# Two tiles of a weight fold laid between the products of neighbouring MLP units, and a planner that lets ScalarE's operations overlap

## The chip, the core and the metric

The kernel runs on one core of one Trainium2 chip. The metric is device microseconds of that core, from the first instruction to the last, inputs and output in HBM. The matrix engine is TensorE (PE in the profile), the others are VectorE (DVE), ScalarE (ACT), GpSimd (POOL) and SyncE (SP), whose queue starts the DMAs.

## What is computed

One token block of 2048 rows and 640 columns passes through a layer norm. On the result stand a linear attention with 32 heads of width 20 and a gated MLP with 1536 hidden columns; both are added to the input.

```python
xn = _layernorm(x)
# A: linear attention; phi is a softmax of p and of -p, side by side
q, k, v = split(xn @ wqkv)                      # 32 heads of 20
pq, pk = q @ w_phi, k @ w_phi                   # per head
phi = concat([softmax(p), softmax(-p)])
kv = einsum("bhsf,bhsd->bhfd", phi_k, v);  z = phi_k.sum(over s)
A = ((phi_q @ kv) / (phi_q @ z + 1e-6)) @ wo
# B: MLP
B = ((silu(xn @ w1)) * (xn @ w3)) @ w2
out = x + A + B
```

## The kernel before

Everything stays on the chip between load and store; the tokens are 16 tiles of 128 rows. The steps of the kernel are written as streams (generators): layer norm (`norms`), transposes, the key fold (`fold_k`), value and key tiles (`attention`), key norms, queries and their followers, MLP units (`mlps`) and output tiles (`outs`). A planner, the loop at the end of the kernel, picks again and again the step that can start first by its own book of due times, and appends its operations to each engine's list. So the order of the work follows from `_Program.commit`, which writes down when each operation ends (`o.end`) and when its engine is free (`self.free`), from fixed costs per operation. Engines run their lists in order and wait for each other by semaphores. A DMA's list is SP's queue.

PSUM has 8 banks, used as four pairs. `banks(2)` gives the pair whose last user ends first, leaving out pairs in `held`.

**The fold.** The per-head matrix `w_phi` is multiplied into the key and query weights, so that a key tile is one projection: `fold_mm(which, dc, k)` makes rows 128 dc to 128 dc + 127 of the folded weight `Wkp` (keys) or `Wqp` (queries) by six products of the transposed weight `wqkT` with the block diagonal `BDc`, four of 140 columns and two of 80, into a bank pair, and copies the pair out (`evac`, to ScalarE or VectorE, whichever the book has free first). One such call is called a fold tile here. `fold_k` issues the key fold's five tiles in a row, and key tiles wait for them (`done["f"]`).

**An MLP unit** (`mlp(b, fc, k)`) computes 128 hidden columns for 512 tokens: five products of 512 columns with `w1` into bank k, five with `w3` into bank k + 1, then ScalarE's `th` (tanh of the first bank), VectorE's `t` (which reads the first bank again) and VectorE's `hT` (which reads `t` and the second bank). There are 48; units 0 to 3 are the first four, before the other weights are loaded.

**A key tile** is ten products of 320 columns with `Wkp` and two exponentials on ScalarE into `ekt`; VectorE then sums and GpSimd scales `ekt`. **A value tile** is ten products with `wv` and one copy on ScalarE. From tile 4 on a value tile follows each key tile (called v tile 4 and so on), and between tiles 9 and 13 a fold tile of the queries follows as well. The layer norm of tiles 4 to 15 is applied (`x_tok`) on VectorE or ScalarE by the book, and SP's DMA transposes bring them into `xnT`, the operand of all projections.

Before the change, the order of TensorE round the fold is: value tiles 0 to 3, units 0 and 1, the five fold tiles, unit 2, key tiles 0 to 3, unit 3, key tile 4, v tile 4, and so on.

Of the kernel before, what the change touches and what calls it, by code (L numbers as in the profile page):

```python
# [3 lines left out]
ACT = mybir.ActivationFunctionType  # L4
ALU = mybir.AluOpType
# [9 lines left out]
DC = D // 128  # L15
# [10 lines left out]
def heads_of_chunk(c):  # L26
    return (128 * c) // DH, (128 * c + 127) // DH
# [16 lines left out]
class _Program:  # L44
# [127 lines left out]
    def commit(self, ops):  # L172
        for o in ops:
            o.idx = len(self.ops)
            o.deps = self.find_deps(o)
            t = self.free[o.eng]
            for d in o.deps:
                t = max(t, d.end + (0.03 if d.eng == o.eng else 0.07))
            o.start = t
            if o.dma:  # L180
                self.free[o.eng] = t + 0.45
                if "T" == o.part:
                    self.free[o.eng] = t + (1.28 if o.cost < 5e5 else o.cost / 105e3)
                self.bus = max(self.bus, t + 0.5) + o.cost / (280e3 if o.part else 305e3)
                if o.part and o.cost > 5e5:
                    self.bus = max(self.bus, self.free[o.eng] + 1.0)
                o.end = self.bus + (1.5 if t < 1 else 1.6 if t < 3.5 or o.part and o.cost < 2e5 else 2.6)
            else:
                o.end = t + o.cost
                self.free[o.eng] = o.end  # L190
            self.ops.append(o)
            if o.eng == "POOL" and not o.dma:
                self.pool = o
            for g in o.reads:
                if isinstance(g, tuple):
                    self.bank.setdefault(g, {})[o.eng] = o
                else:
                    self.last_r.setdefault(g, {})[("dma", o.idx) if o.dma else o.eng] = o
            for g in o.writes:
                if isinstance(g, tuple):  # L200
                    self.bank.setdefault(g, {})[o.eng] = o
                else:
                    self.last_w[g] = o
                    self.last_r.pop(g, None)
# [45 lines left out]
def bass_parallel_sum__linear_kernel_hedgehog__glu_gated_swiglu__prompt_kernel(  # L250
# [29 lines left out]
    def new(name, shape, dtype, offset=None):  # L280
        size = mybir.dt.size(dtype)
        for n in shape[1:]:
            size *= n
        return P.sbuf(name, shape, dtype, region(size) if offset is None else offset)
# [17 lines left out]
    th = new("th", [128, 3, 512], f32)  # L302
    t1 = new("t1", [128, 3, 512], bf)
# [40 lines left out]
    def bank(k, cols=512, off=0, rows=128):  # L344
        return PS[0:rows, k * 512 + off:k * 512 + off + cols]

    def bank2(k, cols):
        return PS[:, k * 512:(k + 2) * 512].rearrange("p (b c) -> p b c", c=512)[:, :, 0:cols]


    def mm(o, l, r, start, stop, shared=False, cost=None):
        n = free(r)
        P.op("PE", "matmul", [o], [l, r], (o, l, r),
             dict(start=start, stop=stop, skip_group_check=shared),
             cost=max(n / 2400 + 0.003, 0.055) if cost is None else cost)
# [5 lines left out]
    def free(ap):  # L361
        n = 1
        for s in ap.shape[1:]:
            n *= s
        return n

    def act(o, i, f, scale=1.0):
        P.op("ACT", "activation", [o], [i], (o, i, f), dict(scale=scale),
             cost=0.17 + free(o) / 1200)
# [5 lines left out]
    def stt(o, a, s, b, f0, f1):  # L375
        P.op("DVE", "scalar_tensor_tensor", [o], [a, b], (),
             dict(out=o, in0=a, scalar=s, in1=b, op0=f0, op1=f1), cost=0.16 + free(o) / 960)

    def copy(eng, o, i, fast=1):
        if eng == "ACT":  # L380
            act(o, i, ACT.Copy)
        else:
            P.op(eng, "tensor_copy", [o], [i], (o, i), cost=0.14 + free(o) / 960 / fast)

    def evac(o, i):

        a = P.free["ACT"] + 0.17 + free(o) / 1200
        d = P.free["DVE"] + 0.14 + free(o) / 960 / (2 if i.dtype == bf else 1)
        copy("ACT" if a <= d else "DVE", o, i, 2 if i.dtype == bf else 1)
# [143 lines left out]
               phi_s[:, c, :].unsqueeze(1).to_broadcast([128, n, DH]),  # L533
               GM[:, c, h0:h1 + 1].unsqueeze(2).to_broadcast([128, n, DH]), ALU.mult)

    def fold_mm(which, dc, k):
        first = [True, True]
        for e in range(DC):
            h0, h1 = heads_of_chunk(e)
            lo, hi = DH * h0, DH * (h1 + 1)  # L540
            for q in range(2):
                a, b = max(lo, 320 * q), min(hi, 320 * q + 320)
                if a < b:
                    mm(bank(k + q, b - a, a - 320 * q), wqkT[:, which * DC + e, 128 * dc:128 * dc + 128],
                       BDc[:, e, a - lo:b - lo], first[q], e == DC - 1 or (q == 0 and e == 2), True)
                    first[q] = False
        dst = (Wqp, Wkp)[which]
        evac(dst[:, dc, :].rearrange("p (b c) -> p b c", c=320), bank2(k, 320))


    def part(w, t, q, i, k, off=0):
        mm(bank(k + q, 320, 0 if q else off), xnT[:, i, t * 128:(t + 1) * 128], w[:, i, 320 * q:320 * q + 320],
           i == 0, i == DC - 1)
# [6 lines left out]
    def v_store(t, k):  # L560
        pv = PS[:, k * 512 + 192:k * 512 + 192 + 60 * NG].rearrange("p (g h c) -> p g h c", h=3, c=DH)
        act(v_heads(v2[:, t, :])[:, :, :, 0:DH], pv, ACT.Copy)

    def v_tile(t, k):
        proj(t, wv, k, 192)
        v_store(t, k)
# [107 lines left out]

    nmlp = [0]

    def mlp(b, fc, k):
        n = nmlp[0] % 3
        nmlp[0] += 1
        for w, kk in ((w1_s, k), (w3_s, k + 1)):  # L680
            for i in range(DC):
                mm(bank(kk), w[:, i, fc * 128:(fc + 1) * 128], xnT[:, i, b * 512:(b + 1) * 512],
                   i == 0, i == DC - 1)
        act(th[:, n, :], bank(k), ACT.Tanh, 0.5)
        stt(t1[:, n, :], th[:, n, :], 1.0, bank(k), ALU.add, ALU.mult)
        stt(hT[b][:, fc, :], t1[:, n, :], 0.5, bank(k + 1), ALU.mult, ALU.mult)

    finish = []
# [26 lines left out]
    held = set()  # L715

    def banks(n):

        def free_at(k):
            return max([o.end for i in range(k, k + n) for o in P.bank.get(("P", i), {}).values()],  # L720
                       default=0.0)
        return min((k for k in range(0, 8, n) if k // 2 not in held), key=free_at)

    done = dict.fromkeys(("w", "ln", "t", "f", "k", "n", "kv", "v", "u", "qp", "qn", "qd", "q", "o", "h", "v0", "bd"), 0)
# [40 lines left out]
            todo = [t, t + 1]  # L765

    def fold_k():
        while not done["bd"]:
            yield None
        for dc in range(DC):  # L770
            yield lambda dc=dc: fold_mm(1, dc, banks(2))
        done["f"] += 1

    done["w"] = 4

# [35 lines left out]
    def attention():  # L811
        def v(t):
            return lambda: v_tile(t, banks(2))

        yield warm_up
        for t in range(4):
            while done["t"] <= t:
                yield None
            k = banks(2)
            held.add(k // 2)  # L820
            for q in range(2):
                for i in range(DC):
                    if t == 0 and q == 1:
                        while done["t"] < 2:
                            yield None
                    yield lambda t=t, q=q, i=i, k=k: part(wv, t, q, i, k, 192)
                    done["v0"] += 1
            yield lambda t=t, k=k: v_store(t, k)
            held.clear()
        while done["f"] < 1:  # L830
            yield None
        for t in range(T):
            while done["t"] <= t:
                yield None
            yield lambda t=t: k_tile(t, banks(2))
            done["k"] = t + 1
            if t >= 4:
                yield v(t)
            if 9 <= t < 14:
                yield lambda dc=t - 9: fold_mm(0, dc, banks(2))  # L840
        yield lambda: P.dma("SP", wo_s[:], A_wo.rearrange("(c p) d -> p c d", p=128))
        done["v"] = 1
# [54 lines left out]
    def o_transposes():  # L897
        for t in range(T):
# [2 lines left out]
            yield lambda t=t: P.dma("SP", oT[:, :, t * 128:(t + 1) * 128], o_tok[:, t % 3, 0:D], True)  # L901
            done["o"] = t + 1

    def mlps():
        for b in range(NB):
            for fc in range(FC):
                while done["t"] < 4 * b + 4 or done["w"] <= fc or b == 2 and done["t"] < T or b == 3 and not done["kv"]:
                    yield None
                yield lambda b=b, fc=fc: mlp(b, fc, banks(2))
                done["u"] = 12 * b + fc + 1  # L910
            done["h"] = b + 1

    def outs():
# [10 lines left out]
    n = len(streams)  # L924
    heads, alive = [None] * n, [True] * n
    while any(alive):
# [32 lines left out]
        i, ops, after = best[2:]  # L959
# [65 lines left out]
```

## Time and profile before

| | |
|---|---|
| time, median of 3 runs | 268.69 us (268.46 to 268.83) |
| the profiled execution | 268.28 us, its span 266.6 us |
| TensorE busy | 261.6 us, 1938 matmul records, 1959 weight loads |
| VectorE, ScalarE, GpSimd busy | 168.8, 98.8, 100.6 us |
| granted TensorE clock | 1.00 throughout |

How to read it: a row of the timeline gives the start and the duration in us, the engine, the line, the operation, output and inputs, and how many operations were merged into it; in brackets stands idle time of the engine before it and what ended it. Nearly every operation is issued by one helper at line 102, so rows are told apart by the names of their tiles: `PS<-BDc,wqkT` is the fold, `PS<-xnT,w_s` an MLP unit, `PS<-Wkp,xnT` a key tile, `PS<-wv,xnT` a value tile. PEld is TensorE's weight load, which goes on beside the products. Matmul ends are modelled and reach over the start of the next one, so distances are taken from start to start; some matmul records are missing.

### The profile page before, as it was taken

What the parts mean: (1) busy time and instruction counts of PE and PEld (TensorE: products, weight loads), DVE (VectorE), ACT (ScalarE), POOL (GpSimd) and SP (SyncE); (2) the same over time, 40 slices, a digit from 0 to 9 for tenths busy, and PEclk for the clock granted to TensorE, in tenths of its full rate; (3) what the DMA queues carried; (4) which work ended last, traced back from release to release, by engine and by line L of the source; (5) the groups of instructions that cost most, each with busy time, mean ns of one, the idle gap of its engine ahead of it and who ended that gap; (6) DMA issues with size and microseconds to landing.
All of it is one profiled execution on the core that took longest, in us unless ns stands there. A gap on an engine that the chain in (4) does not pass through costs nothing.

```text
span 266.6 us, 4793 instructions
## 1 busy us (share of the span) xinstructions
PE 261.6 (98%) x1938; PEld 159.7 (60%) x1959; DVE 168.8 (63%) x293; ACT 98.8 (37%) x196; POOL 100.6 (38%) x143
## 2 busy tenths in 40 slices
PE   8999999999999999999999999999999999999996
PEld 4656677776754555555555555544577777777773
DVE  4569999987766779888888888988512121212112
ACT  5657998888224533443443343322100000000000
POOL 4305669999971344445555444420000000000000
DMA  7998796800092442444444553424212212131201
GB/s 215 299 321 164 169 207 139 271 0 2 12 340 52 79 79 50 87 89 95 79 81 81 100 79 82 92 45 78 49 52 75 74 58 92 52 98 49 91 35 49
DMA packets 63510, 27.73 MB, mean 104 GB/s; under 512 B 49920, under 2 KB 63488, under 8 KB 63488
## 3 DMA queue, kind: packets, MB, share of 16 engines
q1 hardware_dynamic: 62544, 26.90, 42.8%
q10 hardware_dynamic: 944, 0.52, 0.7%
q8 instruction: 15, 0.25, 0.4%
q14 instruction: 7, 0.06, 0.1%
HBM read 12.81 MB, written 2.62 MB: 58 GB/s over the span
## 4 chain that ended last, share of the span: by engine, by line
PE 97%; issue 1%; DVE 1%; POOL 0%
PE PS L102 97%; POOL rstd L102 0%; DVE v L102 0%; DVE bst L102 0%; DVE x_tok L102 0%; DVE xres L102 0%; DVE t L102 0%; DVE mv L102 0%; DVE rstd L102 0%; DVE warm L102 0%
## 5 line engine op out<-in xcount | busy, mean ns | idle before, releaser
L102 PE MATMUL PS<-xnT,w_s 128*128 128x512 bf16 x464 | 105.5, 379 | 1.0 <-ACT Wkp L102 0.2
L102 PEld LDWEIGHTS PS<-xnT,w_s 128*128 128x128 bf16 x480 | 45.7, 98 | 51.1 <-ACT Wkp L102 0.2
L102 PE MATMUL PS<-w_s,hT 128*128 128x320 bf16 (+2 forms) x384 | 54.9, 299 | 0.0
L102 DVE TENSOR_TENSOR xres<-PS,xres 128x640 bf16<-128x640 f32 (+2 forms) x17 | 13.3, 785 | 59.9 <-PE PS L102 59.9
L102 DVE SCALAR_TENSOR_TENSOR t<-th,PS 128x512 bf16<-128x512 f32 x48 | 32.5, 678 | 24.3 <-ACT th L102 24.2
L102 ACT ACTIVATE th<-PS 128x512 f32<-128x512 f32 x48 | 29.3, 611 | 49.4 <-PE PS L102 49.4
L102 PEld LDWEIGHTS PS<-w_s,hT 128*128 128x128 bf16 x384 | 37.1, 98 | 15.1
L102 POOL TENSOR_TENSOR ekt<-ekt,rS 128x640 bf16<-128x640 bf16 x32 | 39.5, 1277 | 0.9 <-DVE rS L102 0.9
L102 ACT ACTIVATE eq<-PS 128x600 bf16<-128x600 f32 (+1 forms) x72 | 23.8, 424 | 29.7 <-PE PS L102 29.7
L102 DVE SCALAR_TENSOR_TENSOR hT<-t,PS 128x512 bf16<-128x512 bf16 x48 | 33.0, 687 | 1.8 <-DVE t L102 0.2
L102 POOL TENSOR_TENSOR rq<-rq,Sq 128x32 f32<-128x32 f32 x16 | 4.1, 254 | 54.9 <-DVE rq L102 54.9
L102 PE MATMUL PS<-wv,xnT 128*128 128x320 bf16 x160 | 24.4, 299 | 0.0
L102 PE MATMUL PS<-wo_s,oT 128*128 128x320 bf16 (+2 forms) x159 | 24.3, 299 | 0.1
L102 PE MATMUL PS<-Wkp,xnT 128*128 128x320 bf16 x160 | 23.9, 299 | 0.0
L102 PE MATMUL PS<-Wqp,xnT 128*128 128x128 bf16 (+1 forms) x156 | 23.3, 297 | 0.3
L102 POOL TENSOR_TENSOR eq<-eq,rq 128x600 bf16<-128x600 bf16 (+1 forms) x32 | 22.6, 728 | 1.2
L102 DVE TENSOR_REDUCE S<-ekt 128x64 f32<-128x1280 bf16 x16 | 23.0, 1438 | 0.0
L102 ACT ACTIVATE ekt<-PS 128x640 bf16<-128x640 f32 x32 | 20.6, 708 | 5.2 <-PE PS L102 5.2
L102 POOL TENSOR_TENSOR half<-eq 128x660 f32<-128x660 bf16 x15 | 20.4, 1358 | 0.6 <-ACT eq L102 0.6
L102 PEld LDWEIGHTS PS<-wo_s,oT 128*128 128x128 bf16 x160 | 15.5, 98 | 6.5
L102 PEld LDWEIGHTS PS<-Wqp,xnT 128*128 128x128 bf16 x160 | 12.9, 98 | 10.5
L102 PEld LDWEIGHTS PS<-Wkp,xnT 128*128 128x128 bf16 x160 | 15.5, 98 | 6.0
(56 smaller groups left out, 178.4 us busy)
## 6 DMA issues: line engine op xcount, KB each, us to landing
w_s<-in_B_w_dram SPq DMA_DIRECT2D x6, 640.0 KB, 6.2
xres<-in_A_x_dram SPq DMA_DIRECT2D x16, 160.0 KB, 2.4
out_dram<-xres SPq DMA_DIRECT2D x15, 160.0 KB, 1.8
x_tok<-in_A_x_dram SPq DMA_DIRECT2D x3, 640.0 KB, 6.4
w_s<-in_B_w_dram SPq DMA_DIRECT2D x1, 1920.0 KB, 8.2
wo_s<-in_A_wo_dram SPq DMA_DIRECT2D x1, 800.0 KB, 7.3
x_tok<-in_A_x_dram SPq DMA_DIRECT2D x3, 160.0 KB, 3.9
wv<-in_A_wqkv_dram ACTq DMA_DIRECT2D x1, 400.0 KB, 3.9
```

The lines of the kernel that those rows point to most:

```text
L102: o = _Op(eng, lambda: m(*args, **kw), r, w, cost)
```

## The change

Fold tile 0 is issued inside unit 1, after all five products with `w1` and three of those with `w3`; fold tiles 1 to 3 are left in a row behind it; fold tile 4 is issued inside unit 2, between its two halves. All five copies of the key fold go to ScalarE by name. An MLP unit now lists `th` and `t` directly behind its first half. Key tiles wait until three units are done, that is, until unit 2 with the last fold tile is out. In the planner's book an operation of ScalarE that costs over 0.2 us leaves the engine free 0.1 us before it ends; its result is still due at the end. The planner then arranges all that follows anew: unit 3 stands ahead of the key tiles and not behind the fourth, nine `x_tok` tiles are on ScalarE where six were, and from the first query tile on, units, query tiles and key/value sums stand in another order.

```diff
             else:
                 o.end = t + o.cost
-                self.free[o.eng] = o.end
+                self.free[o.eng] = o.end - (0.1 if o.eng == "ACT" and o.cost > 0.2 else 0)
...
-    def fold_mm(which, dc, k):
+    def fold_mm(which, dc, k, eng=None):
...
-        evac(dst[:, dc, :].rearrange("p (b c) -> p b c", c=320), bank2(k, 320))
+        o = dst[:, dc, :].rearrange("p (b c) -> p b c", c=320)
+        if eng:
+            copy(eng, o, bank2(k, 320))
+        else:
+            evac(o, bank2(k, 320))
...
-    def mlp(b, fc, k):
+    def mlp(b, fc, k, cut=DC, dc=None):
         n = nmlp[0] % 3
         nmlp[0] += 1
         for w, kk in ((w1_s, k), (w3_s, k + 1)):
             for i in range(DC):
+                if kk > k and i == cut:
+                    held.add(k // 2)
+                    fold_mm(1, dc, banks(2), "ACT")
+                    held.discard(k // 2)
                 mm(bank(kk), w[:, i, fc * 128:(fc + 1) * 128], xnT[:, i, b * 512:(b + 1) * 512],
                    i == 0, i == DC - 1)
-        act(th[:, n, :], bank(k), ACT.Tanh, 0.5)
-        stt(t1[:, n, :], th[:, n, :], 1.0, bank(k), ALU.add, ALU.mult)
+            if kk == k:
+                act(th[:, n, :], bank(k), ACT.Tanh, 0.5)
+                stt(t1[:, n, :], th[:, n, :], 1.0, bank(k), ALU.add, ALU.mult)
         stt(hT[b][:, fc, :], t1[:, n, :], 0.5, bank(k + 1), ALU.mult, ALU.mult)
...
     def fold_k():
-        while not done["bd"]:
+        while done["u"] < 2:
             yield None
-        for dc in range(DC):
-            yield lambda dc=dc: fold_mm(1, dc, banks(2))
-        done["f"] += 1
+        for dc in range(1, DC - 1):
+            yield lambda dc=dc: fold_mm(1, dc, banks(2), "ACT")
+        done["f"] = 1
...
-        while done["f"] < 1:
+        while done["u"] < 3:
             yield None
...
+    CUTS = {1: (3, 0), 2: (0, DC - 1)}
+
     def mlps():
...
-                yield lambda b=b, fc=fc: mlp(b, fc, banks(2))
-                done["u"] = 12 * b + fc + 1
+                n = 12 * b + fc
+                while n == 1 and not done["bd"] or n == 2 and not done["f"]:
+                    yield None
+                if n in CUTS:
+                    yield lambda n=n: mlp(0, n, banks(2), *CUTS[n])
+                else:
+                    yield lambda b=b, fc=fc: mlp(b, fc, banks(2))
+                done["u"] = n + 1
```

## The prediction

> **What bounds the kernel now.** I read the page's first part, then the list of waits of TensorE, then the chain of work that ended last, and last the timeline round the key fold. The page says which engine could be the bound:
>
> ```profile
> span 266.6 us, 4793 instructions
> PE 261.6 (98%) x1938; PEld 159.7 (60%) x1959; DVE 168.8 (63%) x293; ACT 98.8 (37%) x196; POOL 100.6 (38%) x143
> ```
>
> TensorE is busy for 98% of the span. Matmul ends are modelled, so that could still hide small holes. The waits of TensorE (total, times, longest) and the chain of work say how many holes there are:
>
> ```profile
> PE PS L102 <- DVE warm L102: 1.3, 1, 1.3
> PE PS L102 <- ACT Wkp L102: 0.2, 1, 0.2
> ```
>
> ```profile
> 5.65 7.66 PE PS L102 x68
> ...
> 19.33 0.23 issue
> 19.56 7.54 PE PS L102 x49
> 27.10 0.05 issue
> 27.15 36.28 PE PS L102 x279
> ...
> 259.66 4.58 PE PS L102 x33
> ```
>
> TensorE waits for data once before its first product and once, for 0.2 us, on a copy into `Wkp`, the folded key weight. From 19.56 to 264.24 it waits for nobody. The 0.05 us pieces such as the one at 27.10 are no holes: they stand where a matmul's record is missing, as the two groups of the same products show, 464 matmuls against 480 weight loads.
>
> ```profile
> L102 PE MATMUL PS<-xnT,w_s 128*128 128x512 bf16 x464 | 105.5, 379 | 1.0 <-ACT Wkp L102 0.2
> L102 PEld LDWEIGHTS PS<-xnT,w_s 128*128 128x128 bf16 x480 | 45.7, 98 | 51.1 <-ACT Wkp L102 0.2
> ```
>
> So the kernel is bound by the products themselves. No product is added or taken away, and the orders before 13 us and in the last stage are the same in both builds. The change can take away only the hole round the key fold, and it can put new holes anywhere.
>
> **How large the hole is.** The timeline there (start, duration):
>
> ```profile
> 13.37 4.26 PE L102 MATMUL PS<-xnT,w_s 128*128 128x512 bf16 x19
> 15.78 0.69 DVE L102 SCALAR_TENSOR_TENSOR hT<-t,PS 128x512 bf16<-128x512 bf16 x1
> 17.21 0.69 DVE L102 SCALAR_TENSOR_TENSOR t<-th,PS 128x512 bf16<-128x512 f32 x1 [0.75 <-ACT th L102]
> 17.46 1.86 PE L102 MATMUL PS<-BDc,wqkT 128*128 128x140 bf16 x30
> 17.93 0.69 DVE L102 SCALAR_TENSOR_TENSOR hT<-t,PS 128x512 bf16<-128x512 bf16 x1
> 17.98 3.09 ACT L102 ACTIVATE Wkp<-PS 128x640 bf16<-128x640 f32 x5 [0.80 <-PE PS L102]
> 19.33 1.84 PEld L102 LDWEIGHTS PS<-xnT,w_s 128*128 128x128 bf16 x10 [0.19 <-ACT Wkp L102]
> 21.50 5.60 PE L102 MATMUL PS<-Wkp,xnT 128*128 128x320 bf16 x40
> ```
>
> ```profile
> 45.40 0.48 PE L102 MATMUL PS<-BDc,wqkT 128*128 128x140 bf16 x6
> 45.71 0.98 PE L102 MATMUL PS<-Wkp,xnT 128*128 128x320 bf16 x6
> ```
>
> Nineteen 512-wide products go from 13.37 to 17.46, 0.215 each, so an MLP unit (ten) is 2.15 us; the unrecorded first one puts the start of the first unit at 13.15. A fold tile that nobody holds up (the query fold, 45.40 to 45.71) is 0.31, five are 1.56. From the fold's start, 17.46, to the first key tile, 21.50, are 4.04 us, with five fold tiles and one unit in them: 4.04 - 1.56 - 2.15 = 0.33 us lost. The profile names 0.19 of it: unit 2 goes to banks 6 and 7 and waits for ScalarE's copy of fold tile 1. The other 0.14 lies inside the fold: its fourth tile goes to banks 2 and 3, which VectorE's `hT` of unit 1 leaves only at 17.93 + 0.69 = 18.62. The cause of both is five short tiles (0.31 each) in a row whose copies take 3.09 us in all. The largest possible gain is 0.33 us.
>
> **The change part by part.** In the new build TensorE's order is: unit 0, unit 1 with fold tile 0 put in two products before its end, fold tiles 1 to 3, the first half of unit 2, fold tile 4, the second half, unit 3, then key tiles 0 to 4 in a row. Places, counted from 13.15: fold tile 0 at 13.15 + 18 x 0.215 = 17.02, tile 1 at 17.02 + 0.31 + 0.43 = 17.76, tile 3 at 18.38, unit 2 at 18.69, fold tile 4 at 18.69 + 1.08 = 19.77, unit 3 at 21.16, key tile 0 at 23.31. Now each wait that could stand in the way:
>
> *The inputs of fold tile 0*, 0.44 earlier than before. `BDc` has long been there; the transposed key weights were issued at 6.0 and landed 10.2 later at most, at 16.2: 0.8 to spare.
>
> ```profile
> L114 SPq DMA_TRANSPOSE wqkT<-in_A_wqkv_dram x2: 6592/7175/7758, 6.0 to 14.4; - x2
> DMA to landing us min/median/max: 9.8/10.0/10.2
> ```
>
> *The banks.* Fold tile 2 follows unit 0's `hT` (done 16.47). Fold tile 3 takes banks 0 and 1 again behind tile 0's copy. Before, a copy began 0.52 after its tile's first product (17.46 to 17.98), so now at 17.54, and the row of five copies has them 0.6 apart: (3.09 - 0.70)/4. With 0.70 for one the first ends at 18.24, plus 0.05 to be seen, 18.29, against 18.38 less the 0.06 by which a weight load goes ahead: 0.03 to spare. This is the one tight place; I take no wait, with 0.1 as the upper bound. Unit 2's first half needs bank 2, left by `t` at 17.90 against 18.69. Fold tile 4 needs tile 1's copy, about 18.85, against 19.77. Unit 3 needs tile 2's, 19.45, against 21.16; its last copy ends near 21.3, key tile 0 starts at 23.31. Cost of all of these: nothing, with cover of 0.8 us or more but for tile 3. Queued behind the two late copies on ScalarE are only the `th` of units 2 and 3, whose VectorE work is not due before key tile 2 wants banks 2 and 3.
>
> *Unit 3 ahead of the key tiles, and the ScalarE queue.* Before, the unit stood between key tiles 3 and 4 and gave ScalarE 2.15 us for its backlog. Now ScalarE has in order two `x_tok` tiles, key 0, two `x_tok`, keys 1 and 2, one `x_tok`, keys 3 and 4, v 4. The prices:
>
> ```profile
> 23.06 1.30 ACT L102 ACTIVATE ekt<-PS 128x640 bf16<-128x640 f32 x2 [1.50 <-PE PS L102]
> 24.25 2.53 ACT L102 ACTIVATE x_tok<-x_tok,rstd 128x640 bf16<-128x640 bf16 x3
> 26.68 3.66 ACT L102 ACTIVATE ekt<-PS 128x640 bf16<-128x640 f32 x6
> 32.01 0.72 ACT L102 ACTIVATE v<-PS 128x660 bf16<-128x660 f32 x1
> ```
>
> ```profile
> 29.09 1.52 PE L102 MATMUL PS<-Wkp,xnT 128*128 128x320 bf16 x10
> 33.17 1.52 PE L102 MATMUL PS<-wv,xnT 128*128 128x320 bf16 x10
> 38.60 1.52 PE L102 MATMUL PS<-wv,xnT 128*128 128x320 bf16 x10
> ```
>
> Key 0's exponentials began 1.56 after its products (21.50 to 23.06), now at 24.87. Two cost 1.20 when more work follows (1.30 less an overlap of 0.1), an `x_tok` 0.81 (2.53 less 0.1, by three). Key 3 is read when eight exponentials and three `x_tok` are done: 24.87 + 4.80 + 2.43 + 0.10 = 32.20. TensorE needs its banks for v tile 5, at 33.17 - 0.33 = 32.84 now: 0.55 to spare after 0.05 for the signal and 0.04 for the early load. The other steps to 45 us have as much or more. No wait.
>
> *The planner's count.* ScalarE is taken to be free 0.1 us before an operation ends. The rows above say just that: two exponentials in 1.30, six in 3.66. [...] The planner so sees ScalarE free earlier and moves `x_tok` tiles from VectorE to it, and later units, query and key/value steps change places. These all cost the same wherever they stand; only a wait could cost. The order on SP's queue is unchanged, but tiles 12 to 15 are now normalised behind key tile 8's exponentials, near 42.4 (39.96 - 0.33 + 1.56 + 1.20), and their transposes go out at the pace of these four:
>
> ```profile
> 23.88 5.17 SPq L114 DMA_TRANSPOSE xnT<-x_tok  x4
> 39.96 1.52 PE L102 MATMUL PS<-Wkp,xnT 128*128 128x320 bf16 x10
> ```
>
> That is 1.3 each, issued from 43.3 to 48.5, against key tile 12 two rounds (2 x 3.03) behind key tile 10 at 45.71, so 51.4, and tile 15 later still: no wait. POOL's scaling of `ekt` ended at 74.3 + 1.3 = 75.6:
>
> ```profile
> L102 POOL TENSOR_TENSOR ekt<-ekt,rS x32: 1263/1274/1348, 27.7 to 74.3; 128x640 bf16<-128x640 bf16 x32
> DMA to landing us min/median/max: 3.5/3.6/5.0
> 78.42 1.43 PE L102 MATMUL PS<-v,ekt 128*128 128x63 bf16 x44
> ```
>
> The last key/value group, at 78.42, had 2.8 us in hand and moves by 0.3 or less. The second row is the transposing load of a query tile; its issue moves with its tile, and one that slipped by its own spread, 1.4, is my upper bound for a wait there. I take none.
>
> **The sum.** The profiled execution took 268.28, its span is 266.6; minus 0.33 it is 267.95. The median of the runs shown is 268.69, 0.41 above the profiled one; minus 0.33 it is 268.36. Bounds of this case: -0.23 (tile 3 waits 0.1) to -0.33, so 268.36 to 268.46, and about 0.2 of scatter (268.46 to 268.83 before). A measurement of this kernel can tell about 0.2%, 0.54 us, from no change, so this gain lies within what counts as the same.
>
> **The rivals.**
>
> *B, ScalarE falls behind in the row of key tiles.* Without the overlap, eight exponentials at 0.70 and three `x_tok` at 0.92 end at 24.87 + 8.36 = 33.23, and v tile 5 waits 0.5. ScalarE then has key 4, v 4, key 5, two `x_tok` and v 5 to do before v tile 7 gets those banks: 33.23 + 1.40 + 0.72 + 1.40 + 1.84 + 0.72 = 39.31, against 38.60 - 0.33 + 0.5 = 38.77 on TensorE: 0.6 more. Together 1.1 against a gain of 0.33: 268.69 + 0.8 = 269.5. It decides as soon as an operation costs 0.05 more than the rows show (0.55 over eleven). For it: the unit that gave ScalarE time has gone from there. Against it: the rows. Chance 0.07.
>
> *C, a later wait.* The new order of units, query tiles and key/value groups makes one of sixteen query tiles late by 1.4: 268.36 + 1.4, 269.8; half of that gives 269.1. Against it: not one such wait stands in the trace over 180 us, with VectorE, ScalarE and POOL at 63% and less. Chance 0.10, over half of it beyond 0.54.
>
> *D, the wait only moves.* Fold tile 3, or unit 2, waits as long as now. Then the time is 268.69. Only 0.03 of cover at tile 3 speaks for it, but such a wait grows to 0.1, not to 0.33. Chance 0.06.
>
> *E, more than the hole.* Over 0.54 gained. No term gives that: narrow products behind wide ones hide weight loads no better, since a fold tile of 3600/5 = 720 columns takes 0.31 where the wide ones' rate (0.215 for 512) gives 0.30, so five tiles hold 0.05 at most. What is left is scatter on top of 0.33. 268.1 or less, chance 0.17.
>
> The forecast itself has 0.60. Within 0.2%: 0.60, D's 0.06 and 0.04 of C, 0.70. Faster: E, 0.17. Slower: B and 0.06 of C, 0.13. The range goes from 268.0, forecast less scatter, to 269.0, which takes in the bounds, D and small waits of C.
>
> **What would show it right or wrong.** Right: the list of TensorE's waits has only the one before the first product; the key tiles start near 23.3 and v tile 5 near 32.8; the last product starts about 0.3 earlier. Wrong: a row "PE <- ACT ekt" between 30 and 46 us (B), "PE <- DMA eqT" or "<- POOL ekt" later (C), "PE <- ACT Wkp" again (D), or a TensorE stretch that is shorter by more than 0.35 (E).

## The result and the profile after

The changed kernel takes 268.11 us (median of 21 runs, 267.92 to 268.47), the kernel before 268.46 in runs beside it (21 runs). The ratio is 0.9986, with a 95% interval from 0.998 to 0.9993: 0.35 us faster. A second comparison, of twelve runs, gave 268.19 against 268.41 with a ratio of 0.9996 (0.9981 to 1.001), which by itself says nothing. The forecast was a gain of 0.33 us and a time of 268.36; the time came out 0.25 lower, mostly because the kernel before took 268.46 beside it and not the 268.69 of its first three runs.

The page's first part and all waits of TensorE after the change (total, times, longest):

```profile
span 266.4 us, 4813 instructions
PE 262.2 (98%) x1959; PEld 159.4 (60%) x1959; DVE 168.7 (63%) x290; ACT 100.8 (38%) x199; POOL 100.7 (38%) x143
```

```profile
PE PS L102 <- DVE warm L102: 1.3, 1, 1.3
PE PS L102 <- DVE x_tok L102: 0.4, 1, 0.4
```

The wait on `Wkp` is gone, and nothing has come in its place but 0.4 us on the first `x_tok`, before 5.7 us, where the change touches nothing. All 1959 matmuls are recorded this time. The timeline round the fold:

```profile
13.25 4.05 PE L102 MATMUL PS<-xnT,w_s 128*128 128x512 bf16 x18
17.14 0.48 PE L102 MATMUL PS<-BDc,wqkT 128*128 128x140 bf16 x6
17.45 0.59 PE L102 MATMUL PS<-xnT,w_s 128*128 128x512 bf16 x2
17.65 2.64 ACT L102 ACTIVATE Wkp<-PS 128x640 bf16<-128x640 f32 x4 [0.36 <-PE PS L102]
17.88 1.11 PE L102 MATMUL PS<-BDc,wqkT 128*128 128x140 bf16 x18
18.83 1.24 PE L102 MATMUL PS<-xnT,w_s 128*128 128x512 bf16 x5
19.91 0.48 PE L102 MATMUL PS<-BDc,wqkT 128*128 128x140 bf16 x6
20.22 3.40 PE L102 MATMUL PS<-xnT,w_s 128*128 128x512 bf16 x15
23.46 2.74 PE L102 MATMUL PS<-Wkp,xnT 128*128 128x320 bf16 x19
```

From 17.88 to 18.83 three fold tiles take 0.95, which is 3 x 0.31 and no hole. From 13.25 to key tile 0 at 23.46 are 10.21 us, against four units at 2.15 and five tiles at 0.31, 10.15.

Spans don't show this so well, because the start differs from one profile to the next. So each kernel below is also measured from the first product of unit 0 to the start of the last product of all, where the order of the products is the planner's and the sum of their times is the same in every kernel (the mean listed time of each shape, 379 ns for 128x512 and 299 for 128x320 among them, agrees to 1 ns before and after the change). For before and after:

```profile
13.37 0.81 PE L102 MATMUL PS<-xnT,w_s 128*128 128x512 bf16 x3
263.78 0.44 PE L102 MATMUL PS<-w_s,hT 128*128 128x128 bf16 x5
```

```profile
263.81 0.22 PE L102 MATMUL PS<-w_s,hT 128*128 128x128 bf16 x1
```

Before, the first product is the unrecorded one at 13.15, and the last of the five starts four times 0.056 after 263.78, at 264.01: 250.86. After: 263.81 - 13.25 = 250.56. The difference is 0.30, and with the start that was 0.10 later the span is 0.2 shorter. The distance was the same to 0.01 in two profiles of the changed kernel, so it separates kernels that the times do not.

### The profile page after: what moved, and what is told of

It is laid out like the page before. It is cut to its first block, busy times and chain, and to the rows that moved or that the text cites. A ratio compares the mean times of both kernels' runs of the same rounds, so it can differ in the third digit from the quotient of the medians.

```text
span 266.4 us, 4813 instructions
## 1 busy us (share of the span) xinstructions
PE 262.2 (98%) x1959; PEld 159.4 (60%) x1959; DVE 168.7 (63%) x290; ACT 100.8 (38%) x199; POOL 100.7 (38%) x143
## 4 chain that ended last, share of the span: by engine, by line
PE 96%; DMA 2%; DVE 1%; SPq 0%; POOL 0%; issue 0%
PE PS L102 96%; DMA x_tok<-in_A_x_dram 2%; SPq L114 0%; POOL rstd L102 0%; DVE bst L102 0%; DVE x_tok L102 0%; DVE xres L102 0%; DVE rstd L102 0%
## 5 line engine op out<-in xcount | busy, mean ns | idle before, releaser
L102 PE MATMUL PS<-xnT,w_s 128*128 128x512 bf16 x480 | 107.4, 379 | 0.0
L102 PE MATMUL PS<-Wqp,xnT 128*128 128x512 bf16 (+1 forms) x160 | 24.3, 299 | 0.0
L102 PEld LDWEIGHTS PS<-wv,xnT 128*128 128x128 bf16 x160 | 15.4, 98 | 6.1 <-ACT xnT L102 0.2
```

The source lines that it names most:

```text
L102: o = _Op(eng, lambda: m(*args, **kw), r, w, cost)
```

## The experiments

The theory is the prediction's: the gain is the hole at the fold, and the rest of the new order costs and brings nothing. The main rival is that the planner's new count, with the order that follows from it, brings the gain. Times are against runs of the kernel before on the same chip. An interval is some 0.1% to either side, so 0.1 us is read from the trace, 0.5 us from the times. The ratio is formed from the single runs and need not be that of the two medians. The places alone had 5 runs, the two insertions 11 each, the other experiments 12. One of the runs of the last insertion took 985.77 us and is not in its ratio.

| kernel | us (before beside it) | ratio, 95% interval | distance |
|---|---|---|---|
| before | | | 250.86 |
| changed | 268.11 (268.46) | 0.9986 (0.998 to 0.9993) | 250.56 |
| count alone | 268.39 (268.41) | 1.0005 (0.9996 to 1.0013) | 250.86 |
| places alone | 269.85 (268.41) | 1.0052 (1.004 to 1.0064) | 252.25 |
| first insertion only | 268.21 (268.41) | 0.9992 (0.9984 to 1.0001) | 250.58 |
| last insertion only | 268.37 (268.41) | 1.0001 (0.9992 to 1.001) | 250.75 |
| tile 0 one product later | 268.31 (268.39) | 0.9998 (0.9989 to 1.0008) | 250.68 |
| one ScalarE operation more | 268.27 (268.39) | 0.9993 (0.9985 to 1.0001) | 250.55 |
| three more | 269.05 (268.39) | 1.0032 (1.0015 to 1.0048) | 251.50 |
| places alone, third sum later | 268.90 (268.41) | 1.0018 (1.0009 to 1.0026) | 251.23 |
| overlap counted as 0.2 | 269.08 (268.41) | 1.0023 (1.0014 to 1.0032) | 251.42 |
| changed, again | 268.19 (268.41) | 0.9996 (0.9981 to 1.001) | 250.55 |

### The two halves of the change alone

The count alone, on the kernel before:

```diff
-                self.free[o.eng] = o.end
+                self.free[o.eng] = o.end - (0.1 if o.eng == "ACT" and o.cost > 0.2 else 0)
```

> The fold as before, five tiles in a row, but ScalarE booked free 0.1 us before an operation ends, so the planner arranges the rest anew. Theory (hole): the same two waits at the fold, 0.3 us in all (8.35 us from the first product of unit 0 to key tile 0), no others; time that of before within 0.15 us. Rival (planner's count): 0.3 us or more under before, with the hole still there.

The distance is that of before, 250.86, and the list of waits has the old entry:

```profile
PE PS L102 <- ACT Wkp L102: 0.2, 1, 0.2
```

The rival falls: the new count by itself brings nothing. The new places alone, in the changed kernel:

```diff
-                self.free[o.eng] = o.end - (0.1 if o.eng == "ACT" and o.cost > 0.2 else 0)
+                self.free[o.eng] = o.end
```

> The new fold places, but ScalarE is booked free at the end of each operation as before. Theory (the gain is the hole at the fold, 0.33 us): no wait on Wkp or hT between 13 and 24 us; from the first product of unit 0 to key tile 0, unit 3 not counted, 8.03 us where before had 8.35; time 0.3 to 0.4 us under before. Rival (the gain comes from the planner's new count and the order that it leads to): the time is that of before, within 0.15 us, or the plan leaves a wait of its own between 40 and 49 us, where the old count takes ScalarE for the bound.

The hole at the fold is gone, and yet this kernel is 1.4 us slower than before. Neither theory had that. Its waits of TensorE:

```profile
PE PS L102 <- DVE warm L102: 1.3, 1, 1.3
PE PS L102 <- POOL ekt L102: 0.9, 1, 0.9
PE PS L102 <- DVE x_tok L102: 0.6, 1, 0.6
PE PS L102 <- DMA eqT<-eq: 0.5, 1, 0.5
```

The two new ones, on GpSimd's scaled `ekt` and on a query transpose, stand here in the timeline:

```profile
64.50 3.94 PE L102 MATMUL PS<-v,ekt 128*128 128x63 bf16 x131
69.30 0.19 PE L102 MATMUL PS<-v,ekt 128*128 128x42 bf16 x1 [0.86 <-POOL ekt L102]
...
84.76 0.49 PE L102 MATMUL PS<-KVc,eqT 128*128 128x63 bf16 x11 [0.49 <-DMA eqT<-eq]
```

All three key/value groups of token tiles 0 to 11 stand in a row behind query tile 0, 132 products, and only the last of them waits. It does not wait for tile 11, whose scaling ended at 68.01. In the kernel it reads 128 columns of `ekt` from column 1200 of tile 11's 1280, so 48 columns of tile 12 as well, and GpSimd scales the first half of tile 12 just then, until 69.24:

```profile
67.97 1.27 POOL L102 TENSOR_TENSOR ekt<-ekt,rS 128x640 bf16<-128x640 bf16 x1
```

In the changed kernel query tile 1 stands in between, and GpSimd is earlier. The query wait has a second part: the transpose was issued at 79.57, 2.0 later than in the changed kernel, and took 5.1 us to land, where the median of these transposes is 3.6; at 3.6 it would have been there at 83.2, before TensorE came to it at 84.1. Two rows on `ekt`, first of the kernel with the places alone, then of the changed one:

```profile
L102 ACT ACTIVATE ekt<-PS x32: 679/704/767, 26.4 to 62.6; 128x640 bf16<-128x640 f32 x32
L102 POOL TENSOR_TENSOR ekt<-ekt,rS x32: 1267/1272/1351, 29.9 to 76.6; 128x640 bf16<-128x640 bf16 x32
```

```profile
L102 ACT ACTIVATE ekt<-PS x32: 695/708/843, 25.0 to 62.5; 128x640 bf16<-128x640 f32 x32
L102 POOL TENSOR_TENSOR ekt<-ekt,rS x32: 1267/1275/1352, 29.0 to 74.5; 128x640 bf16<-128x640 bf16 x32
```

With the places alone key tile 0's exponentials come 1.4 us later, and GpSimd's last scaling starts 2.0 later (76.56 against 74.53). The rows of ScalarE ahead of these exponentials and VectorE's sum of key tile 1, again first with the places alone, then of the changed kernel, show where it begins:

```profile
23.15 3.34 ACT L102 ACTIVATE x_tok<-x_tok,rstd 128x640 bf16<-128x640 bf16 x4
33.09 1.43 DVE L102 TENSOR_REDUCE S<-ekt 128x64 f32<-128x1280 bf16 x1
```

```profile
23.07 1.72 ACT L102 ACTIVATE x_tok<-x_tok,rstd 128x640 bf16<-128x640 bf16 x2
30.90 1.43 DVE L102 TENSOR_REDUCE S<-ekt 128x64 f32<-128x1280 bf16 x1
```

The old count puts four `x_tok` tiles ahead of key tile 0's exponentials, the new one two. VectorE's sum of key tile 1 then comes 2.2 later, GpSimd's scaling of that tile 2.0, and the 2.0 stay to the end. The distance, 252.25, is 1.69 above the changed kernel's.

To see how much of it is the place of the third group, the same kernel with that group held back:

```diff
         for t in range(0, T, 4):
+            while t == 8 and done["u"] < 5:
+                yield None
             yield lambda t=t: part(t)
```

> The kernel with the new fold places and the old book (which was 1.4 us slower than before), with one edit: the third group of key/value sums (token tiles 8 to 11) may not be issued before five MLP units are done, so that it stands behind two units and not directly behind the second group. Theory (that loss is one misplaced step: the book of then has 1 us of TensorE waits near 45 us that do not occur, so TensorE comes to this group before GpSimd has scaled tile 11, which there ends near 69.3, and the first query product comes ahead of its transpose): neither wait is left; time 0.25 to 0.4 us under before, 1.7 under the kernel without this edit. Rival (GpSimd's chain, 2 us later there than in the changed kernel, is itself the bound): the waits only move to the fourth group or to the query products; time still 0.5 us or more over before.

Neither fits whole. What ends near 69.3 in the kernel with the places alone is tile 12's first half, not tile 11. Of the 1.69, 1.02 are gone (252.25 to 251.23), and so is the wait on the transpose. But the time is 0.49 over before, where the theory had 0.25 to 0.4 under, and a wait on GpSimd is left, now at the fourth group, as the rival had it:

```profile
77.71 0.34 PE L102 MATMUL PS<-v,ekt 128*128 128x63 bf16 x6 [0.50 <-POOL ekt L102]
```

The planner has also moved this group: it starts at 75.95 here, and at 77.16, without a wait, in the kernel with the places alone. So both were at work: groups issued too early, and a GpSimd chain that is 2.0 us late. By the rows either would have sufficed for the first wait: 2.0 earlier, tile 12's half would be done at 67.2, before TensorE came to the product at 68.3, and in the changed kernel's order TensorE comes to it only at 69.56. This is worked out and not run. Why the old count puts four `x_tok` tiles there was not taken apart further.

### How much each insertion carries

The first insertion only, with fold tiles 1 to 4 in a row:

```diff
-        for dc in range(1, DC - 1):
+        for dc in range(1, DC):
...
-    CUTS = {1: (3, 0), 2: (0, DC - 1)}
+    CUTS = {1: (3, 0)}
```

The last insertion only, with fold tiles 0 to 3 in a row:

```diff
-        for dc in range(1, DC - 1):
+        for dc in range(DC - 1):
...
-    CUTS = {1: (3, 0), 2: (0, DC - 1)}
+    CUTS = {2: (0, DC - 1)}
```

> The changed kernel, but only fold tile 0 is put into unit 1; tiles 1 to 4 follow in a row and unit 2 is whole. Theory (hole, by the steps of the prediction): tile 0's copy starts 0.4 us earlier, so unit 2's banks (6 and 7, behind tile 1's copy) come free at about 18.9 against a first weight load at 18.9 to 19.0, and fold tile 4's bank 3 (behind unit 1's hT, done near 18.7) just in time: between 0 and 0.1 us of the hole left, time 0.25 to 0.35 us under before. Rival (both insertions carry half each): 0.15 us of the hole left, time 0.15 to 0.2 under before.

> The changed kernel, but only fold tile 4 is put into unit 2; tiles 0 to 3 stand in a row behind unit 1. Theory (hole): tile 3 goes to banks 2 and 3 and still waits for unit 1's hT, 0.12 to 0.15 us; unit 2 takes banks 0 and 1, whose copy ends in time. 0.14 us of the hole left, time 0.15 to 0.2 us under before. Rival (the whole gain is the wait on Wkp that the list of waits names, 0.2): nothing left at the fold, time 0.33 under before.

The first insertion does nearly all: the distance is 250.58, 0.02 to 0.03 above the changed kernel, and no wait at the fold is listed. Tile 4 in the middle of unit 2 is worth those 0.03 us. With the last insertion only, 0.19 of the hole is left, the copy is no longer waited for, and the weight loads wait for unit 1's `hT`, as the prediction read from the order of the rows without a wait being named:

```profile
17.65 1.32 PEld L102 LDWEIGHTS PS<-BDc,wqkT 128*128 128x128 bf16 x21
18.41 0.69 DVE L102 SCALAR_TENSOR_TENSOR hT<-t,PS 128x512 bf16<-128x512 bf16 x1
19.15 0.15 PEld L102 LDWEIGHTS PS<-BDc,wqkT 128*128 128x128 bf16 x3 [0.18 <-DVE hT L102]
```

(`hT` ends at 18.41 + 0.69 = 19.10, the next load starts at 19.15.) I had put 0.14 there. The ratio's intervals of both kernels include no change, so the split rests on the traces.

### The covers that the prediction counted on

The tight place was fold tile 3, which takes the banks of tile 0. One product later for tile 0:

```diff
-    CUTS = {1: (3, 0), 2: (0, DC - 1)}
+    CUTS = {1: (4, 0), 2: (0, DC - 1)}
```

> The changed kernel with fold tile 0 one product of unit 1 later (after four of the five with w3). By the prediction fold tile 3 had 0.03 us to spare behind tile 0's copy, by the trace of the changed kernel 0.05. Theory (that cover is real): the copy comes 0.215 us later and tile 3's place does not move, so TensorE waits 0.15 to 0.2 us on Wkp near 18.5; time 0.15 to 0.2 us over the changed kernel. Rival (slack elsewhere takes it up, the place in the unit is free): no wait, the time of the changed kernel.

The distance grows by 0.12 to 250.68, all of it in one gap at fold tile 3. It is too short for the list of waits; the weight load there waits 0.13 for `Wkp`. A place of 0.215 later less 0.05 to spare would be 0.165; the cover was 0.09. It is real and thin, and the place in the unit is not free. The times (268.31 against 268.39) cannot tell this kernel from before or from the changed one.

The other cover was ScalarE's queue in the row of key tiles. Operations that nobody reads, put into the finished lists so that no order changes, behind the second exponential of key tile 0 (with `added < 3`, of key tiles 1 and 2 too):

```diff
+            if seen % 2 == 0 and added < 1:
+                added += 1
+                j, i = xres[:, added, 0:512], xnT[:, 0, 0:512]
+                w = _Op("ACT", lambda j=j, i=i: nc.scalar.activation(j, i, ACT.Copy, scale=1.0), [], [], 0.5)
...
+                P.ops.insert(P.ops.index(p) + 1, w)
```

> The changed kernel with one more ScalarE operation of 512 columns, whose result nobody uses, behind key tile 0's exponentials; all orders else as in the changed kernel. It adds 0.5 us to ScalarE's queue ahead of key tile 3's exponentials, which v tile 5's banks wait for. Theory (v tile 5 has 0.48 to 0.5 us to spare): no wait or one of under 0.1 us near 32.8; time that of the changed kernel. Rival (the cover is thinner than the rows say, or ScalarE's later steps lose it): a wait of 0.2 us or more.

> The same with three such operations, behind the exponentials of key tiles 0, 1 and 2: 1.5 us more ahead of key tile 3's. Theory (cover of 0.5 us, then one for one): TensorE waits about 1.0 us on ekt at v tile 5, and no more than 0.2 behind it, since all later steps are then 1.0 later themselves; time 1.0 us over the changed kernel, so 0.65 over before. Rival (ScalarE takes it up in its idle time): under 0.4 us in all.

One more costs nothing: the distance is 250.55. Three more cost 0.95, in one wait at v tile 5:

```profile
31.87 1.52 PE L102 MATMUL PS<-Wkp,xnT 128*128 128x320 bf16 x10
34.16 1.53 PE L102 MATMUL PS<-wv,xnT 128*128 128x320 bf16 x10 [0.78 <-ACT ekt L102]
35.53 1.52 PE L102 MATMUL PS<-Wkp,xnT 128*128 128x320 bf16 x10
```

Key tile 5 starts at 31.87 and v tile 5 should 1.36 later, at 33.23; it starts at 34.16. Behind it every step is in time again. That is the forecast of a cover of about half a microsecond and one for one beyond it: each added operation delays the next by 0.52 in this trace, three by 1.56, so the cover was 1.56 - 0.95 = 0.61. The time is 0.66 over before, 0.65 was expected.

### The amount of the overlap

```diff
-                self.free[o.eng] = o.end - (0.1 if o.eng == "ACT" and o.cost > 0.2 else 0)
+                self.free[o.eng] = o.end - (0.2 if o.eng == "ACT" and o.cost > 0.2 else 0)
```

> The changed kernel with ScalarE booked free 0.2 us before an operation ends, twice what the timeline shows. Theory (the amount only picks an order; what counts is that no wait comes out of it): no hole at the fold, waits of TensorE after 13 us only where the new order has a step too early, of which the likeliest are query products behind their transposes; time that of the changed kernel within 0.3 us. Rival (a book that is wrong by 0.1 costs as much as it did in the other direction): 1 us or more over the changed kernel.

The mechanism was as expected, its size and place were not: a wait on the copy of a query fold tile,

```profile
47.98 0.48 PE L102 MATMUL PS<-BDc,wqkT 128*128 128x140 bf16 x6
49.12 1.12 PE L102 MATMUL PS<-Wkp,xnT 128*128 128x320 bf16 x7 [0.66 <-ACT Wqp L102]
```

and a short one on `ekt` near 34 put the distance at 251.42, 0.87 above the changed kernel, and the time 0.67 over before. The key tile should follow the fold tile after 0.31, at 48.29, and starts 0.83 later. Here the book frees ScalarE too early, and TensorE arrives before ScalarE is done. The 0.87 lies between the theory's 0.3 and the rival's 1.

### The changed kernel again

> The changed kernel itself, for a second profile and times beside the other two. Theory: no wait on TensorE after 13 us, again; 0.3 to 0.45 us under before. The waits ahead of 13 us (on x_tok and the first loads) differ from profile to profile by some tenths of a us and are no part of the change.

The distance is 250.55, and no wait after 13 us is listed. The time was 0.22 under before, less than expected, within a wide interval. In this profile unit 0 starts at 13.54.

## Why the prediction was right

*What bounds the kernel.* Right. Between 13 us and the last product TensorE pauses only at the waits named above; each difference between two distances is such a wait.

*The size of the hole.* Forecast 0.33, the trace gives 0.30, the times 0.35. The two causes were as read: the count alone keeps both, and the last insertion alone keeps only the one on `hT`. That one was put at 0.14; start to start it cost 0.11 in the kernel before, with 0.18 for the copy, and 0.19 where it stood alone. The sums of the prediction are a little short in the changed kernel too, which has no wait (10.16 to key tile 0, 10.21 in the trace), so the missing 0.03 most likely lies in the sizes 2.15 and 0.31.

*The places.* Fold tile 0 was put 3.87 us after unit 0's start, key tile 0 10.16, v tile 5 19.69. The trace after has 3.89, 10.21 and 32.97 - 13.25 = 19.72 (the row of v tile 5 below). Tile 3's cover of 0.03 was near 0.1 by experiment.

*The ScalarE queue.* Right, and tested. The queue and TensorE in the changed kernel:

```profile
30.98 2.51 ACT L102 ACTIVATE ekt<-PS 128x640 bf16<-128x640 f32 x4
32.97 1.52 PE L102 MATMUL PS<-wv,xnT 128*128 128x320 bf16 x10
```

Key tile 3's two exponentials are the first of the four and end near 32.3 (0.6 apart, 0.7 for one), where 32.20 was forecast for a start at 13.15, which is 32.30 for this one. Rival B did not come, and the added operations put the point from which ScalarE is late between 0.5 and 1.5 us of extra work. In the first row above, exponentials of 0.7 us begin 0.6 apart ((2.51 - 0.70)/3), so the listed times of two in a row overlap by 0.1 us, which is what the new count takes; the 269.5 that rival B drew from operations without overlap did not come.

*Rivals C to E.* None came in the changed kernel. But the prediction had one step too few: it said that the planner's later steps cost the same wherever they stand and gave a late wait 0.10, without asking what the new places do under the old count. There late waits do come, for 1.7 us in two places, and the overlap of 0.2 brings one of 0.8. That the changed kernel's own order has none does not follow from the prediction's argument; that part was luck in some measure, although the product that waits with the places alone has 2.3 us in hand there (69.56 against 67.21). The new count brings none of the gain, but in these runs no gain came without it.

*The chances.* The measured 0.13% lies within the 0.2% that had 0.70. The ratio's interval over 21 runs excludes no change, so a small gain is there.

## What to carry to other kernels

Where the bounding engine waits almost nowhere, sum its holes first: they are the most that a new order can bring, and here the sum was right to 0.03 us. Short steps with long copies (fold tiles of 0.31 us, copies that began 0.60 apart) go better between long steps here; moving just the first of a row by two products was nearly enough (0.28 of the 0.30 us), since it starts the chain of copies 0.43 us earlier. When a planner decides the rest of the order, run the planner's change and the local change apart: one brought nothing, the other alone lost 1.4 us, and together they gained 0.3. And look at what a waiting operation reads: a product that read 48 columns too far waited 1.0 us for a tile that it had no use for.

## What was not expected of the hardware

The start scatters more than the change is worth. Unit 0's first product came between 12.98 and 13.84 us over twelve profiles, while the distance behind it repeated to 0.01 us for the same program. In the two profiles below VectorE waits for the third token tile's load, 0.18 and 0.53 us, and the second tile's normalisation stands behind that wait, at 7.06 and 7.35. The first statistics of the third tile, in the changed kernel's first profile (unit 0 at 13.25) and in its second (13.54):

```profile
5.77 0.49 DVE L102 BATCH_NORM_STATS2 bst<-x_tok 128x6 f32<-128x320 bf16 x1 [0.18 <-DMA x_tok<-in_A_x_dram]
```

```profile
6.12 0.49 DVE L102 BATCH_NORM_STATS2 bst<-x_tok 128x6 f32<-128x320 bf16 x1 [0.53 <-DMA x_tok<-in_A_x_dram]
```

And in these traces the duration of a ScalarE operation is not its price in a queue. The copy of a value tile is listed with 0.72 us before the change. In the kernel with an overlap of 0.2, where the queue was full, three in a row are listed with 0.85, 0.88 and 0.91, and the next operation still began 0.60 us behind each of them, as here:

```profile
45.95 0.91 ACT L102 ACTIVATE v<-PS 128x660 bf16<-128x660 f32 x1
46.55 1.92 ACT L102 ACTIVATE x_tok<-x_tok,rstd 128x640 bf16<-128x640 bf16 x2
```
